# Another written order in the first segment, and other slots and pairs in the attention steps

## The chip, the cores and the metric

The kernel runs on one core of one Trainium2 chip. The time is device microseconds of that core. TensorE (PE) multiplies, VectorE (DVE), ScalarE (ACT) and GpSimd (POOL) do the elementwise work, and SyncE (SP) issues nearly all transfers. Each engine works through its own instructions in a fixed order, and an instruction that waits holds up everything behind it on that engine.

## What is computed

One transformer block with 2048 tokens of width 1024, in float32, whose two norms are modulated by a condition c:

```python
mod = (silu(c) @ w_mod).reshape(6, 1, 1024)          # sa, ca, ga, sb, cb, gb
h = layernorm(x) * (1 + ca) + sa
x = x + ga * attention(h)
h = layernorm(x) * (1 + cb) + sb
x = x + gb * ((gelu(h @ w_gate) * (h @ w_up)) @ w_down)
```

The attention has 32 heads of 32 and goes through the tokens in four segments s of 512. In each segment, with phi(t) = t + 1 for t > 0 and exp(t) else:

```python
a_dot = softmax(qs @ ks.T * scale + mask) @ vs       # within the segment, causal
a_mem = phi(qs) @ M / (phi(qs) @ z + 1e-6)           # from the segments before
o = g * a_mem + (1 - g) * a_dot                      # g = sigmoid(beta), per head
M = M + phi(ks).T @ vs ; z = z + sum(phi(ks))
```

Then o @ wo. So a segment reads the memory M, z that the segments before it have left.

## The kernel before

**Products.** A float32 operand is cut into a high part, rounded to the fp32r type that PE takes at full speed, and a low part, the remainder. A product is three fp32r matmuls: high by high, low by high, high by low. The names carry this: kh and kl, qh and ql, hha and hla, and w with two halves. ACT writes the high part, DVE or GpSimd subtracts for the low part (`split_w` does it for weights, GpSimd in four pieces of 256 columns).

**Steps.** The attention has 32 steps n = (half hf, head group g of 4 heads, segment s). In step n PE computes the scores S and the memory M of step n, the projections v, k, q of step n + 1 (`kv_part`, `q_part`) and the values (T, O, R) of step n − 1. What stands after what on PE is set by a string of 31 letters:

```python
ORDER = "K N K K V K V N K K V V K N V K S Q S V V Q S Q A S K M Q V V"
```

Each letter advances one generator to its next yield; a letter's position is called its slot. Besides, a list `todo` of (slot, function) has weight loads, weight cuts and columns done at a slot; a slot beyond the end falls into the next step. PE's order is exactly this written order. In the first segment (`start`) the order of all engines is the written one. In the steps the other engines' order is set by a scheduler, which places an instruction when it reckons it ready; `behind=True` keeps an instruction in written order on its engine.

**A step's pieces.** q leaves PSUM three ways: qh (ACT), ql (DVE, from qh), and for s > 0 phi(q) = pq (ACT exp into eq, DVE min, DVE max and add). k likewise into kh, kl and kn, whose transposes kT give pk = phi(k). v goes through vr (ACT) and the transposes vT into vx. The two PSUM banks named mm serve v, k and q in turn. kh, kl, qh, ql are sent by SP into ks and qs, 96 rows for the three matmul terms. S is masked and its row maximum taken by DVE (sj, mm), exponentiated for the sum by ACT (sj). The maxima go through a DVE transpose (tt) into rows 96 to 128 of qs, so that T = ks' qs comes with the maximum subtracted; ACT takes its exp (pt), GpSimd masks it, and O follows. rx and ry are the factors of the two parts: rx from the sums (ACT), ry from the memory's denominator (DVE), num is phi(q) by mz, the masked memory.

**Columns.** The modulation vector's rows 16 to 47 are computed in the steps, one or two per step: SP loads 128 rows of w_mod into a raw tile (`mod_load`, four raw tiles serve all loads), and one DVE instruction of 1024 elements (`mod_col`, L146) multiplies and sums them into a column of modT. In the first segment the columns that the first norm needs are made partly so and partly by PE (`mod_rows`, `mod_cols`).

**The first segment** normalises segment 0 on the chip: statistics per tile of 128 tokens on DVE, the power on GpSimd, scale on ACT and DVE, transposes on PE (`turn`), modulation on ACT (`high`), low part on DVE (`low`), then the products for q, k, v of step 0 k-tile by k-tile (`products`). The same is begun for segment 1 (x1), whose eight k-tiles `norm_seg` then finishes in step 0. `warm` issues matmuls whose result nobody reads.

## Time and profile before

| | us |
|---|---|
| median of 3 runs | 2773.78 |
| lowest and highest | 2773.21 and 2775.84 |
| the profiled execution | 2774.15 |
| its span | 2772.4 |
| PE busy in it | 2729.2 (98%) |
| DVE, ACT, POOL busy | 1767.3, 1287.7, 535.4 |

A row of a timeline has its start in us from the span's beginning, its duration in us, the engine, the line of the program, the instruction, what it writes from what, and in brackets how long the engine stood idle before it and what ended that. Neighbours on one engine overlap by a little, since the end of an instruction lies in the start of the next; the distance between starts is what an instruction costs its queue. A row of waits has the waiting instruction, what ended the wait, the total, the number and the longest. The first segment reaches to about 65 us, the steps to about 970 us, and the feed-forward part, which the change leaves alone, fills the rest.

### The profile page before, as it was taken

To read this page: it belongs to the slowest core of one execution; us is meant where nothing else is said; L and a number is where in the kernel's file an instruction comes from. 1 tells how busy PE (TensorE), PEld (TensorE's weight loads), DVE (VectorE), ACT (ScalarE), POOL (GpSimd) and SP (SyncE) were. 2 spreads that over 40 slices of the span, in tenths; PEclk is the share of its full clock that TensorE was granted. 3 is DMA by queue.
4 is the path that set the end of the run, shared out by engine and by line. 5 is a ranking of instruction groups with operands and counts; after the bars stand their busy time and mean duration, and the time that the engine had idled before them with its cause. 6 is when DMAs were issued, how large, how long until landed. Compare 5 with 4: busy or idle time off the path is not lost.

```text
span 2772.4 us, 38550 instructions
## 1 busy us (share of the span) xinstructions
PE 2729.2 (98%) x13336; PEld 2206.0 (80%) x13336; DVE 1767.3 (64%) x3723; ACT 1287.7 (46%) x2855; POOL 535.4 (19%) x972
## 2 busy tenths in 40 slices
PE   7999999999999999999999999999999999999999
PEld 5777777777777777788888887888888888888887
DVE  7565657767566754777776768667778754434552
ACT  6788866767676735334443324233223243232221
POOL 1333333333333521100000002000000002012442
PEclk9999999999999999999999999999999999999999
DMA  7666656665555657656555754333567595544652
GB/s 258 123 145 150 148 111 131 146 140 126 115 111 99 155 176 247 200 205 219 208 208 183 245 176 156 122 145 143 190 239 254 214 315 176 183 139 155 199 197 80
DMA packets 229748, 480.18 MB, mean 173 GB/s; under 512 B 17456, under 2 KB 92464, under 8 KB 229552
## 3 DMA queue, kind: packets, MB, share of 16 engines
q1 hardware_dynamic: 229408, 477.58, 57.3%
q8 instruction: 105, 1.72, 0.3%
q14 instruction: 91, 0.75, 0.1%
q10 hardware_dynamic: 144, 0.13, 0.0%
HBM read 300.96 MB, written 126.35 MB: 154 GB/s over the span
## 4 chain that ended last, share of the span: by engine, by line
PE 86%; DVE 6%; issue 2%; DMA 2%; ACT 2%; POOL 0%; SPq 0%; DVEq 0%; ACTq 0%; POOLq 0%
PE f L1286 36%; PE d L1457 19%; PE k L318 6%; PE q L318 5%; PE y L790 4%; PE v L318 3%; PE S L658 3%; PE O L731 3%; PE T L722 3%; DVE qs L675 1%; PE M L638 1%; DVE sj L660 1%; PE R L745 1%; PE num L696 1%; PE vT L334 0%
## 5 line engine op out<-in xcount | busy, mean ns | idle before, releaser
L1286 PE MATMUL f<-A,B 128*128 128x512 f32 x4704 | 1074.6, 390 | 4.8 <-DVE c L1251 3.2
L1286 PEld LDWEIGHTS f<-A,B 128*128 128x128 f32 x4704 | 882.3, 188 | 190.5 <-issue 2.9
L1457 PE MATMUL d<-wb,ah 128*128 128x512 f32 x2352 | 534.2, 389 | 0.2 <-DVE wb L1337 0.2
L1457 PEld LDWEIGHTS d<-wb,ah 128*128 128x128 f32 x2352 | 441.3, 188 | 92.7 <-DVE wb L1337 0.6
L660 DVE CUSTOM_DVE_ANT_0 sj<-S,mask 128x384 f32<-128x384 f32 (+3 forms) x512 | 227.8, 487 | 183.1 <-PE S L658 174.4
L662 ACT ACTIVATE sj<-sj,mm 128x384 f32<-128x384 f32 (+3 forms) x512 | 282.3, 556 | 28.1 <-DVE mm L660 26.0
L724 ACT ACTIVATE pt<-T 128x256 f32<-128x256 f32 (+3 forms) x512 | 184.9, 457 | 116.8 <-PE T L722 111.9
L725 POOL TENSOR_SCALAR_AFFINE_SELECT pt<-pt 128x128 f32<-128x128 f32 x512 | 168.3, 347 | 338.1 <-ACT pt L724 331.0
L1337 DVE TENSOR_TENSOR ah<-ar,ah 128x1792 fp32r<-128x1792 f32 x56 | 116.4, 2079 | 171.0 <-ACT ah L1336 163.5
L1336 ACT ACTIVATE ah<-ar 128x1792 fp32r<-128x1792 f32 x56 | 95.3, 1702 | 274.1 <-PE d L1457 248.2
L1253 ACT ACTIVATE g<-g 128x512 f32<-128x512 f32 x56 | 35.4, 632 | 302.8 <-DVE g L1253 302.8
L160 POOL TENSOR_TENSOR w<-r,w 128x256 fp32r<-128x256 f32 x180 | 133.1, 771 | 165.3 <-ACT w L155 144.9
L924 DVE TENSOR_TENSOR B<-t,B 128x512 fp32r<-128x512 f32 x168 | 116.1, 691 | 56.4 <-ACT B L927 56.3
L1362 POOL TENSOR_TENSOR yo<-u,gbb 128x256 f32<-128x256 f32 x32 | 30.0, 970 | 547.6 <-ACT gbb L132 547.6
L927 ACT ACTIVATE B<-t 128x512 fp32r<-128x512 f32 x168 | 105.5, 628 | 63.8 <-PE f L1286 60.0
L790 PE MATMUL y<-wo,hho 128*128 128x512 f32 x384 | 125.8, 393 | 0.5 <-DVE xr L794 0.5
L722 PE MATMUL T<-qs,ks 128*128 128x256 f32 (+2 forms) x512 | 115.0, 339 | 7.3 <-DVE qs L675 2.6
L722 PEld LDWEIGHTS T<-qs,ks 128*128 128x128 f32 x512 | 82.9, 188 | 48.4 <-issue 21.7
L1250 ACT ACTIVATE g<-f 128x512 f32<-128x512 f32 x56 | 33.5, 598 | 176.5 <-PE f L1286 176.5
L1380 POOL TENSOR_TENSOR xo<-xo,yo 128x256 f32<-128x256 f32 x64 | 71.8, 1151 | 210.7 <-DMA xo<-x_d 161.6
L924 DVE TENSOR_TENSOR B<-rg,B 128x512 fp32r<-128x512 f32 x112 | 78.2, 699 | 52.4 <-ACT B L927 52.2
L658 PE MATMUL S<-ks,qs 96*128 96x256 f32 (+2 forms) x512 | 108.3, 333 | 0.8 <-DVE mm L660 0.8
(251 smaller groups left out, 4326.5 us busy)
## 6 DMA issues: line engine op xcount, KB each, us to landing
ar<-hid_d SPq DMA_DIRECT2D x56, 896.0 KB, 5.1
rg<-wg SPq DMA_DIRECT2D x56, 512.0 KB, 4.6
ru<-wu SPq DMA_DIRECT2D x56, 512.0 KB, 5.4
hid_d<-g SPq DMA_DIRECT2D x56, 512.0 KB, 3.0
sc<-hid_d SPq DMA_DIRECT2D x56, 512.0 KB, 5.6
hid_d<-sc SPq DMA_DIRECT2D x56, 512.0 KB, 3.0
...
```

Source lines behind the costliest of these rows:

```text
L160: eng.tensor_sub(w[:, 1, k:k + 256], r[:, k:k + 256], f32(w[:, 0, k:k + 256]))
L318: nc.tensor.matmul(ps, w[:, a], b, start=(kt == 0 and a == 0 and b is hi), stop=(kt == KT - 1 and a == 1))
L658: nc.tensor.matmul(ps[:, :nk], qs[:96, j, i * P:(i + 1) * P], ks[:96, j, :nk], start=True, stop=True)
L660: nc.vector.tensor_tensor_reduce(out=sj[:, :nv], in0=ps[:, :nv], in1=mask[:, L - nv:], scale=-1.0, scalar=3.4e38, op0=ALU.add, op1=ALU.min ...
L662: nc.scalar.activation(sj[:, :nv], sj[:, :nv], AF.Exp, bias=mm[:, j, i:i + 1], scale=-1.0, accum_out=ll[:, i, j:j + 1])
L722: nc.tensor.matmul(ps[:, :nn], ks[:, j, kc * P:(kc + 1) * P], qs[:, j, L - nn:], start=True, stop=True)
L724: nc.scalar.activation(pt, ps[:, nn - n:nn], AF.Exp)
L725: nc.gpsimd.affine_select(pt[:, :P], pt[:, :P], pattern=[[1, P]], compare_op=ALU.is_ge, fill=0.0, base=0, channel_multiplier=-1)
L790: nc.tensor.matmul(ps, b[:, i * P:(i + 1) * P], w[:, a, g % 2], start=(g == 0 and a == 0 and b is hi), stop=(g == G - 1 and a == 1))
L924: eng.tensor_sub(dst[:, k], a[:, k], b[:, k])
L1286: nc.tensor.matmul(ps, B[m, i][:, a, kt * P:(kt + 1) * P], A[p, i, kt][b], start=(start and kt == 0 and a == 0 and b == 0), stop=(kt == 3 ...
L1457: nc.tensor.matmul(ps[t], ops[n][:, x, k, t * P:(t + 1) * P], b[:, y, kk % 2], start=(kk == 0 and x == 0 and y == 0), stop=(kk == 13 and x ...
```

## The change

Five things are edited.

1. In `start` the order is another. The statistics of tile 0 come ahead of the diagonal that spreads the condition, scales of segment 0 go to ACT in six of eight cases (four before), the cut of wv stands behind the modulation rows, k-tile 6 comes ahead of 4 and 5, and the four statistics of segment 1 stand together with the scales behind them. Ahead of k-tile 2 stand two warming matmuls where three were, and six more follow the last product. kl and ql are written after v's copy.
2. GpSimd's order in the first two steps is the written one.
3. In `k_out` kn comes ahead of kl, and in `q_out` eq ahead of ql.
4. `memory` yields after mz, and the string has one M more ahead of the third Q, so that mz is written there.
5. Weight cuts and loads have other slots (14, 19, 26, 37 become 15, 20, 24, 31), and a column comes 23 slots after its load and not 14.

Left out of the diff are helpers that only carry this (`stats`, `shift`, `scale` are the old statements one by one, and `SC` gets its entries in either order).

```diff
@@ -334,15 +336,19 @@
             nc.tensor.transpose(ps[:, t * P:(t + 1) * P], vr[:, t * P:(t + 1) * P], ident)
         nc.vector.tensor_copy(vx[:, :, :P], ps.rearrange("p (t m) -> p t m", m=P))
 
-    def k_out(s, nm, ps):
+    def k_low(kh, kl, ps):
+        nc.vector.tensor_sub(kl, ps, f32(kh))
+
+    def k_out(s, nm, ps, low=k_low):
         kh = t2("kh" + nm, "sp", bufs=4, dt=F32R)
         kl = t2("kl" + nm, "sp", bufs=4, dt=F32R)
         nc.scalar.activation(kh, ps, AF.Copy)
-        nc.vector.tensor_sub(kl, ps, f32(kh))
         kr = None
         if s < NSEG - 1:
             kr = t2("kn" + nm, "kn")
             nc.scalar.activation(kr, ps, AF.Copy)
+        if low:
+            low(kh, kl, ps)
         return kh, kl, kr
 
     def k_send(n, kh, kl, kr):
@@ -365,12 +371,13 @@
         qh = t2("qh" + nm, "sp", bufs=4, dt=F32R)
         ql = t2("ql" + nm, "sp" if n else "sj", bufs=4 if n else 3, dt=F32R)
         nc.scalar.activation(qh, ps, AF.Copy, scale=SCALE)
+        if s > 0:
+            e = tmp_tile("eq" + nm)
+            nc.scalar.activation(e, ps, AF.Exp)
         nc.vector.scalar_tensor_tensor(ql, ps, SCALE, f32(qh), op0=ALU.mult, op1=ALU.subtract)
         qs = t2("qs" + nm, "qs", bufs=2, dt=F32R, shape=(P, 4, L))
         pq = None
         if s > 0:
-            e = tmp_tile("eq" + nm)
-            nc.scalar.activation(e, ps, AF.Exp)
             nc.vector.tensor_scalar_min(e, e, 1.0)
             pq = t2("pq" + nm, "pq", bufs=2)
             nc.vector.scalar_tensor_tensor(pq, ps, 0.0, e, op0=ALU.max, op1=ALU.add)
@@ -472,32 +478,24 @@
...
-        def normal(halves, name, engs):
-            st = []
-            for i in range(4):
-                if i > 1:
-                    scale(i - 2, halves, *st[i - 2], name, engs)
-                st.append(norm_stats([halves[0][i], halves[1][i]], f"{name}{i}"))
-                yield
-            for i in (2, 3):
-                scale(i, halves, *st[i], name, engs)
-
-        for i, _ in enumerate(normal(x0, "a0", (nc.scalar, nc.vector))):
-            if i in (2, 3):
-                next(row)
...
@@ -555,14 +553,36 @@
                 for kt in kts:
                     mm(i, ps[i], 0, 0, kt)
 
+        (xa, xb), dve = x0, nc.vector
+        stats(0, 0, x0)
+        next(row)
+        shift(0, 0)
+        scale(xa[0], 0, 0)
+        scale(xb[0], 0, 0)
+        stats(0, 1, x0)
+        stats(0, 2, x0)
+        shift(0, 1)
+        scale(xa[1], 0, 1)
+        scale(xb[1], 0, 1)
+        stats(0, 3, x0)
+        shift(0, 2)
+        scale(xa[2], 0, 2)
+        nc.vector.tensor_reduce(sel4, pick, axis=AX.X, op=ALU.add)
+        nc.vector.tensor_copy(blk.rearrange("p (j e) -> p j e", e=DH), sel4.unsqueeze(2).to_broadcast([P, 4, DH]))
+        shift(0, 3)
+        scale(xa[3], 0, 3)
+        scale(xb[2], 0, 2, dve)
+        scale(xb[3], 0, 3, dve)
+        for _ in row:
+            pass
         warm(1)
-        cut(1)
         mod_rows(0, 0)
+        turn(0)
+        turn(1)
         warm(1)
         mod_rows(0, 1)
+        cut(1)
         warm(1)
-        turn(0)
-        turn(1)
         mod_cols(0)
         for d in range(4):
             nc.sync.dma_start(spare[d], wms[1, d])
@@ -576,7 +596,7 @@
         cut(0)
         turn(2)
         turn(3)
-        warm(3)
+        warm(2)
         high(2)
         mods(3)
         low(2)
@@ -585,43 +605,54 @@
         nc.sync.dma_start(bb, bass.AP(tensor=beta.tensor, offset=beta.offset, ap=[[0, P], [1, H]]))
         x1 = [fetch(x[L + i * P:L + (i + 1) * P, :], f"x1_{i}") for i in range(4)]
         x1h = [[t[:, h * L:(h + 1) * L] for t in x1] for h in range(2)]
-        norm = normal(x1h, "a1", (nc.vector, nc.scalar))
         products(0, 1)
         mod_rows(1, 0)
         products(2)
         high(3)
         low(3)
+        turn(6)
+        mods(6)
         mod_rows(1, 1)
+        high(6)
         turn(4)
+        mod_cols(1)
         turn(5)
-        mod_col(*got[6][0])
-        mod_cols(1)
         high(4)
-        mod_col(*got[6][1])
         products(3)
         high(5)
-        low(4)
-        turn(6)
         mod_col(*got[7][0])
-        low(5)
-        high(6)
+        low(6)
         mod_col(*got[7][1])
-        low(6)
-        products(4)
         turn(7)
         high(7)
-        next(norm)
+        products(6)
+        low(4)
+        low(5)
+        stats(1, 0, x1h)
+        low(7)
+        stats(1, 1, x1h)
+        shift(1, 0)
+        scale(x1h[0][0], 1, 0)
+        scale(x1h[1][0], 1, 0)
+        products(4)
         products(5)
-        low(7)
-        products(6, 7)
-        next(norm)
-        kk = k_out(0, nm, ps[2])
+        products(7)
+        stats(1, 2, x1h)
+        shift(1, 1)
+        scale(x1h[0][1], 1, 1)
+        stats(1, 3, x1h)
+        shift(1, 2)
+        kk = k_out(0, nm, ps[2], None)
+        warm(6)
+        scale(x1h[0][2], 1, 2)
+        shift(1, 3)
+        scale(x1h[0][3], 1, 3)
+        for i in range(1, 4):
+            scale(x1h[1][i], 1, i, dve)
+        vv = v_out(0, nm, ps[1])
+        k_low(*kk[:2], ps[2])
         k_send(0, *kk)
         q_out(0, 0, nm, ps[0])
-        next(norm)
-        vv = v_out(0, nm, ps[1])
-        for _ in norm:
-            pass
         k_turn(0, 0, nm, *kk)
         v_turn(nm, *vv)
         sigmoid(gall, bb)
@@ -690,7 +721,7 @@
             mz = t2("mz" + nm, "mz", bufs=1, shape=(P, P + 4))
             nc.vector.tensor_mul(mz[:, :P], M[:, :P], blk)
             nc.vector.tensor_scalar_mul(mz[:, P:], sel4, M[:, P:P + 1])
-
+            yield
             ps = [s_ps(f"num{nm}_{i}").rearrange("p (i m) -> p i m", i=2)[:, :, :P + 4] for i in range(2)]
             for i in range(4):
                 nc.tensor.matmul(ps[i // 2][:, i % 2], pq[:, i * P:(i + 1) * P], mz, start=True, stop=True)
@@ -1491,7 +1522,7 @@
 
 
     steps = [(hf, g, s) for hf in range(2) for g in range(G) for s in (2 * hf, 2 * hf + 1)]
-    ORDER = "K N K K V K V N K K V V K N V K S Q S V V Q S Q A S K M Q V V"
+    ORDER = "K N K K V K V N K K V V K N V K S Q S V V Q M S Q A S K M Q V V"
     ORDER0 = "N N N N N N N N K K K K S K S K S K A S K Q Q Q K M Q"
     none = iter(())
     todo = []
@@ -1504,7 +1535,11 @@
             norm_1 = start()
         norm_a = norm_tiles(x, hT_d, (2, 3), 1, 0, "a")
         next(norm_a)
+        firsts = ExitStack()
+        firsts.enter_context(tc.manual_schedule(engines={mybir.EngineType.Pool}))
         for n in range(len(steps) + 1):
+            if n == 2:
+                firsts.close()
             work = {k: none for k in "VSAMKQN"}
             if n > 0:
                 work["V"] = values(n - 1, *steps[n - 1][1:])
@@ -1526,7 +1561,7 @@
             else:
                 work["K"] = work["Q"] = proj
             if n + 2 < len(steps) and n % 2 == 0:
-                weights(*steps[n + 2][:2], [(4, 0, 1), (8, 0, 2), (14, 1, 1), (19, 1, 2), (26, 0, 0), (37, 1, 0)])
+                weights(*steps[n + 2][:2], [(4, 0, 1), (8, 0, 2), (15, 1, 1), (20, 1, 2), (24, 0, 0), (31, 1, 0)])
             if n == 30:
                 rs = {}
 
@@ -1542,7 +1577,7 @@
                 for pos in (20, 27)[:1 + (15 <= n < 20)]:
                     got = []
                     todo.append((pos, lambda r=rest.pop(0), got=got: got.append(mod_load(r))))
-                    todo.append((pos + 14, lambda got=got: mod_col(*got[0], behind=True)))
+                    todo.append((pos + 23, lambda got=got: mod_col(*got[0], behind=True)))
             for pos, q in enumerate((ORDER if n else ORDER0).split()):
                 for f in [f for at, f in todo if at == pos]:
                     f()
```

DVE at the end of the first segment, from ql and the scales of segment 1 (rx here, with their statistics sta, mva, rsa and shifts mra) on. Before:

```order
L341 TENSOR_TENSOR kl0_0_504<-k0_0_241,kh0_0_503 128x512
L368 SCALAR_TENSOR_TENSOR ql0_0_513<-q0_0_242,qh0_0_512 128x512
L480 TENSOR_SCALAR mra1_0_520<-mva10_460,rsa10_464 128x1
L484 TENSOR_SCALAR rx1_0_333<-rx1_0_333,rsa10_464,mra1_0_520 128x512
L191 BN_STATS sta12_524<-rx1_2_337 128x6 x2
L194 BN_AGGR mva12_525<-sta12_524 128x2
L196 TENSOR_SCALAR rsa12_529<-mva12_525 128x1
L480 TENSOR_SCALAR mra1_1_536<-mva11_496,rsa11_500 128x1
L484 TENSOR_SCALAR rx1_1_335<-rx1_1_335,rsa11_500,mra1_1_536 128x512
L191 BN_STATS sta13_540<-rx1_3_339 128x6 x2
L194 BN_AGGR mva13_541<-sta13_540 128x2
L196 TENSOR_SCALAR rsa13_545<-mva13_541 128x1
```

With the change:

```order
L489 TENSOR_SCALAR mra1_1_514<-mva1_1_468,rsa1_1_472 128x1
L193 BN_STATS sta1_3_517<-rx1_3_338 128x6 x2
L196 BN_AGGR mva1_3_518<-sta1_3_517 128x2
L198 TENSOR_SCALAR rsa1_3_522<-mva1_3_518 128x1
L489 TENSOR_SCALAR mra1_2_525<-mva1_2_507,rsa1_2_511 128x1
L489 TENSOR_SCALAR mra1_3_540<-mva1_3_518,rsa1_3_522 128x1
L495 TENSOR_SCALAR rx1_1_334<-rx1_1_334,rsa1_1_472,mra1_1_514 128x512
L495 TENSOR_SCALAR rx1_2_336<-rx1_2_336,rsa1_2_511,mra1_2_525 128x512
L495 TENSOR_SCALAR rx1_3_338<-rx1_3_338,rsa1_3_522,mra1_3_540 128x512
L340 TENSOR_TENSOR kl0_0_528<-k0_0_181,kh0_0_527 128x512
L377 SCALAR_TENSOR_TENSOR ql0_0_555<-q0_0_182,qh0_0_554 128x512
L365 TENSOR_SCALAR ek0_0_567<-ek0_0_567 128x512
```

kl and ql stood ahead of the first scale, and each scale stood between two sets of statistics. Now the statistics of all four tiles are through first (the first two lie further up), then the last shifts, three scales, and only then kl and ql.

ACT at the end of a step of the first half, where q of group 1, segment 1 is taken out of PSUM (pt are the exponentials of step 1, 0). Before:

```order
L358 ACTIVATE ek1_1_1630<-kT1_1_1625 128x512
L367 ACTIVATE qh1_1_1641<-q1_1_1493 128x512
L682 ACTIVATE rx1_0_1618<-rc1_0_1615 128x512
L373 ACTIVATE eq1_1_1646<-q1_1_1493 128x512
L724 ACTIVATE pt1_0_00_1695<-T1_0_00_1693 128x512
```

With the change:

```order
L364 ACTIVATE ek1_1_1639<-kT1_1_1634 128x512
L373 ACTIVATE qh1_1_1650<-q1_1_1502 128x512
L376 ACTIVATE eq1_1_1653<-q1_1_1502 128x512
L713 ACTIVATE rx1_0_1629<-rc1_0_1626 128x512
L755 ACTIVATE pt1_0_00_1709<-T1_0_00_1707 128x512
```

eq stood between rx and the first pt; now it stands ahead of rx, right behind qh.

DVE at the end of a step of the second half, around pq of group 2, segment 2 (wm38 is a column, mz2_2 the small part of the masked memory, vx2_3 the next values). Before:

```order
L368 SCALAR_TENSOR_TENSOR ql2_2_7993<-q2_2_7840,qh2_2_7992 128x512
L753 TENSOR_TENSOR R1_2_7877<-R1_2_7877,Y1_2_8005 128x512
L146 ISA wm38_7875,modT_108<-wm38_7875,scb_110 128x1024
L146 ISA modT_108 128x1
L374 TENSOR_SCALAR eq2_2_7997<-eq2_2_7997 128x512
L151 TENSOR_SCALAR modT_108<-modT_108 128x1
L692 TENSOR_SCALAR mz2_2_8333<-sel4_100,Mt2_1_2738 128x4
L376 SCALAR_TENSOR_TENSOR pq2_2_8000<-q2_2_7840,eq2_2_7997 128x512
L335 COPY vx2_3_8064<-vT2_3_8101 128x4x128
```

With the change:

```order
L377 SCALAR_TENSOR_TENSOR ql2_2_8002<-q2_2_7847,qh2_2_8001 128x512
L381 TENSOR_SCALAR eq2_2_8004<-eq2_2_8004 128x512
L784 TENSOR_TENSOR R1_2_7886<-R1_2_7886,Y1_2_8014 128x512
L383 SCALAR_TENSOR_TENSOR pq2_2_8009<-q2_2_7847,eq2_2_8004 128x512
L723 TENSOR_SCALAR mz2_2_8267<-sel4_100,Mt2_1_2750 128x4
L337 COPY vx2_3_8071<-vT2_3_8108 128x4x128
L146 ISA wm38_7884,modT_108<-wm38_7884,scb_110 128x1024
L146 ISA modT_108 128x1
L151 TENSOR_SCALAR modT_108<-modT_108 128x1
```

The column wm38 stood ahead of eq and pq; now it stands behind vx, and pq follows two rows after eq.

More of the change, by code (lines that the diff above doesn't have):

```diff
@@ L151, in mod_col, with split_w @@
             nc.vector.tensor_scalar_add(modT[:, r:r + 1], modT[:, r:r + 1], 1.0)
-    def split_w(r, w, eng=nc.gpsimd):
-        nc.scalar.activation(w[:, 0], r, AF.Copy)
+    def split_w(r, w, eng=nc.gpsimd, behind=False):
+        i = nc.scalar.activation(w[:, 0], r, AF.Copy)
+        if behind:
+            tc.keep_in_program_order(i)
         if eng is nc.vector:
@@ L307, in cut @@
         def cut(i):
-            W[g][i] = split_w(raws[i], wsp_tile(f"w{i}_{half}_{g}"))
+            W[g][i] = split_w(raws[i], wsp_tile(f"w{i}_{half}_{g}"), behind=False)
         for pos, f, i in at:
@@ L472, in warm, with stats, shift, scale @@
                 nc.tensor.matmul(ps[:, :2 * P], ones, mask[:, :2 * P], start=True, stop=True)
-        nc.vector.tensor_reduce(sel4, pick, axis=AX.X, op=ALU.add)
-        nc.vector.tensor_copy(blk.rearrange("p (j e) -> p j e", e=DH), sel4.unsqueeze(2).to_broadcast([P, 4, DH]))
-        def scale(i, halves, mv, rs, name, engs):
-            mr = cs([P, 1], f"mr{name}_{i}", tag="mr", bufs=4)
-            nc.vector.tensor_scalar(mr, mv[:, 0:1], rs, -1.0, op0=ALU.mult, op1=ALU.mult)
-            for h in range(2):
-                t = halves[h][i]
-                if engs[h] is nc.vector:
-                    nc.vector.tensor_scalar(t, t, rs, mr, op0=ALU.mult, op1=ALU.add)
-                else:
-                    nc.scalar.activation(t, t, AF.Identity, bias=mr, scale=rs)
-        def normal(halves, name, engs):
-            st = []
-            for i in range(4):
-                if i > 1:
-                    scale(i - 2, halves, *st[i - 2], name, engs)
-                st.append(norm_stats([halves[0][i], halves[1][i]], f"{name}{i}"))
-                yield
-            for i in (2, 3):
-                scale(i, halves, *st[i], name, engs)
-        for i, _ in enumerate(normal(x0, "a0", (nc.scalar, nc.vector))):
-            if i in (2, 3):
-                next(row)
+        st = {}
+        def stats(s, i, halves):
+            st[s, i] = norm_stats([halves[0][i], halves[1][i]], f"a{s}_{i}")
+        def shift(s, i):
+            mv, rs = st[s, i]
+            mr = cs([P, 1], f"mra{s}_{i}", tag="mr", bufs=4)
+            nc.vector.tensor_scalar(mr, mv[:, 0:1], rs, -1.0, op0=ALU.mult, op1=ALU.mult)
+            st[s, i] = rs, mr
+        def scale(t, s, i, eng=nc.scalar):
+            rs, mr = st[s, i]
+            if eng is nc.vector:
+                nc.vector.tensor_scalar(t, t, rs, mr, op0=ALU.mult, op1=ALU.add)
+            else:
+                nc.scalar.activation(t, t, AF.Identity, bias=mr, scale=rs)
         w0 = W[0] = [None] * 3
@@ L543, in high @@
             nc.scalar.activation(hi[kt][1], h, AF.Copy)
-        hT[0] = []
+        hT[0] = [None] * KT
         def low(kt):
@@ L682, in scores @@
         nc.scalar.activation(rx, rc.unsqueeze(3).to_broadcast([P, 4, 4, DH]), AF.Copy)
-        SC[n] = [rx, None]
+        SC.setdefault(n, [None, None])[0] = rx
     def memory(n, g, s):
```

4 lines of the change are left out of this document (2 added, 2 removed).

## The prediction

> **What bounds the kernel now.** I read the windows by stage first, to see where TensorE stands still at all.
>
> ```profile
> 40.00:60.00 20.00, 14.85 (x76) 12.00 (x76) 16.15 (x40) 13.02 (x22) 2.67 (x7) 0.91 0.68 94
> ...
> 300.00:600.00 300.00, 293.82 (x1710) 230.47 (x1709) 198.41 (x661) 212.84 (x614) 112.40 (x249) 1.00 0.64 138
> 600.00:970.00 370.00, 363.52 (x2096) 283.69 (x2095) 247.44 (x829) 256.00 (x734) 138.15 (x302) 1.00 0.58 120
> 970.00:2772.00 1802.00, 1790.10 (x7964) 1475.65 (x7962) 1125.83 (x1614) 591.45 (x938) 195.78 (x208) 1.00 0.55 191
> ```
>
> The columns are the stretch, its length, then busy time of PE, weight load, DVE, ACT, POOL, the granted clock, DMA share and GB/s. After 970 us, where the change touches nothing, PE is full. Between 40 and 60 it idles 5.15 us, and through the attention steps some 6 us in 300 and again in 370. So the kernel is bound by TensorE, and only its stalls can be won. Then the list of PE's waits, for who ends them:
>
> ```profile
> PE k L318 <- ACT vr L325: 3.4, 7, 0.5
> PE tpa L282 <- DVE rx L484: 3.2, 3, 2.0
> ...
> PE T L722 <- DVE qs L675: 2.6, 4, 0.8
> PE T L722 <- DVE ry L704: 2.4, 5, 0.9
> ...
> PE T L722 <- ACT pt L724: 1.7, 3, 0.8
> ...
> PE kT L356 <- ACT kn L345: 1.3, 1, 1.3
> ...
> PE k L318 <- DVE pq L376: 0.7, 2, 0.3
> ```
>
> Each row gives the total, the number of waits and the longest. None is large; the change aims at the queues of ACT and DVE behind six of them, so I take them one by one.
>
> **The first segment: its beginning loses.** These are ACT and, last, DVE between 17 and 20 us:
>
> ```profile
> 17.57 1.06 ACT L155 ACTIVATE w<-rw 128x1024 fp32r<-128x1024 f32 x1 [1.02 <-DMA rw<-wv]
> 18.53 0.58 ACT L519 ACTIVATE mr<-md 128x512 f32<-128x512 f32 x1
> 20.57 0.78 ACT L541 ACTIVATE h<-tpa,modT 128x512 f32<-128x512 f32 x1 [1.47 <-DVE modT L526]
> 18.66 1.23 DVE L157 TENSOR_TENSOR w<-rw,w 128x1024 fp32r<-128x1024 f32 x1 [2.38 <-ACT w L155]
> ```
>
> Before, the cut of wv (1.06 on ACT, 1.23 on DVE) runs while PE still makes the modulation rows. The change puts that cut behind mr, and eight transposes ahead of the second half of the rows. By my reckoning mr then starts at 18.35 (18.53 now), the cut at 18.85, its DVE half at 19.95, and modT, behind it on DVE, at 21.2; the first h goes from 20.57 to 21.45. Some of this 0.9 is made up, since the order of the eight k-tiles is better packed; I carry 0.6 to the last product, with 0 and 0.9 as bounds.
>
> **Its end gains.** The timelines of ACT, DVE and PE around the start of segment 1:
>
> ```profile
> 45.51 0.60 ACT L345 ACTIVATE kn<-k 128x512 f32<-128x512 f32 x1 [0.83 <-DVE kl L341]
> 54.32 1.49 ACT L284 ACTIVATE h<-tpa,modT 128x512 f32<-128x512 f32 x2
> ...
> 40.94 1.28 DVE L191 BATCH_NORM_STATS2 sta<-rx 128x6 f32<-128x512 f32 x2
> ...
> 50.27 1.28 DVE L191 BATCH_NORM_STATS2 sta<-rx 128x6 f32<-128x512 f32 x2
> ...
> 51.90 0.20 DVE L480 TENSOR_SCALAR mra<-mva,rsa 128x1 f32<-128x1 f32 x1
> ...
> 53.00 0.55 DVE L484 TENSOR_SCALAR rx<-rx,rsa,mra 128x512 f32<-128x512 f32 x1
> ...
> 65.50 0.65 PE L658 MATMUL S<-ks,qs 96*128 96x256 f32 x4
> ```
>
> Now the last scale of the next segment's tokens ends at 53.55, because kl, ql and the scales stand between the statistics on DVE. After the change the four statistics follow each other from about 41.5 (40.94 and the 0.6 lost above), each 1.63 long (50.27 to 51.90), with one hla (0.6) and small shifts (0.9) between, then three scales of 0.46: the end is at about 51, and ACT, which has the other half of each tile and waits for the last shift only, comes to its first h at 51.7 instead of 54.32: a gain of 2.6. From there to the first S at 65.50 the chain is ACT's two passes over each of eight k-tiles, unchanged, so S moves up by the same 2.6. The cover of that is the transfer of q: ql is sent some 5 us later than now, and I expect the last qs to land about 1.2 us before S asks for it. If it came 2 us later, 0.8 would be lost. The six extra warming matmuls fall where PE waits anyway.
>
> In step 0 two more stalls go:
>
> ```profile
> 80.06 0.60 ACT L345 ACTIVATE kn<-k 128x512 f32<-128x512 f32 x1 [1.18 <-DVE kl L341]
> 84.16 0.60 ACT L373 ACTIVATE eq<-q 128x512 f32<-128x512 f32 x1 [0.76 <-DVE ql L368]
> 90.32 0.44 PE L722 MATMUL T<-qs,ks 128*128 128x384 f32 x1 [0.69 <-ACT pt L724]
> ```
>
> kn and eq need only the product in PSUM, but the program makes ACT wait for the DVE subtraction written ahead of them. With kn straight behind kh its 1.3 us on PE (the kT row above) goes. eq 0.76 earlier brings the normalisation of the next tokens forward as well, and of the T stall of 0.69 I count 0.4 as won. The first segment and step 0: 2.6 + 1.3 + 0.4 = **4.3 won**; bounds 2 and 6.
>
> **k behind pq (A).** Nine times k waits 0.3 to 0.5 by the list. The lateness is more, since the ends of matmuls are modelled:
>
> ```profile
> 608.92 0.87 PE L722 MATMUL T<-qs,ks 128*128 128x384 f32 x4
> 609.62 0.40 PE L318 MATMUL k<-hhh,w 128*128 128x512 f32 x1
> ...
> 636.76 0.69 PE L722 MATMUL T<-qs,ks 128*128 128x384 f32 x3
> 637.91 0.50 PE L318 MATMUL k<-hhh,w 128*128 128x512 f32 x1 [0.46 <-ACT vr L325]
> ...
> 635.58 1.27 DVE L146 CUSTOM_DVE_ANT_0 wm<-wm,scb 128x1024 f32<-128x1024 f32 x1
> 637.39 0.68 DVE L376 SCALAR_TENSOR_TENSOR pq<-q,eq 128x512 f32<-128x512 f32 x1
> ...
> 647.08 0.29 DVE L660 CUSTOM_DVE_ANT_0 sj<-S,mask 128x128 f32<-128x128 f32 x1 [3.29 <-PE S L658]
> ```
>
> Undisturbed, four T take 0.70 to the next k; three would put k at 637.28, and it starts at 637.91: 0.6 late. k needs one of two PSUM banks, the one that q leaves when pq has read it, or the one that v leaves with vr. pq stands behind a column of 1.27 on DVE, so the program gave k the bank of v. In the change the column stands behind pq and vx, k gets the bank of q everywhere, and pq, 1.2 us earlier, ends near 636.8, 0.5 before k asks. Nine times 0.6 is **5.4 won**; nothing at the other end, if pq only exchanges the column for another delay.
>
> **T behind qs (B).**
>
> ```profile
> 316.30 2.71 DVE L675 TENSOR_SCALAR qs<-tt,seli 32x512 fp32r<-32x512 f32 x4
> 317.12 3.46 POOL L160 TENSOR_TENSOR w<-r,w 128x256 fp32r<-128x256 f32 x4 [5.11 <-ACT w L155]
> 490.89 1.69 DVE L675 TENSOR_SCALAR qs<-tt,seli 32x512 fp32r<-32x512 f32 x4
> ```
>
> The four qs take 1.69 alone and 2.71 beside GpSimd's part of a weight cut. In two steps eq now goes ahead of that cut on ACT, GpSimd starts 0.5 later, and about half of the 0.8 stall goes: 1.0. In a third a column leaves the chain to qs, and the whole 0.9 goes. In the fourth the cut only moves from before rx to before pt and wins nothing. Together **1.9**, bounds 0 and 2.6.
>
> **T behind pt (C).** In seven steps eq stands between rx and the first pt and waits for ql:
>
> ```profile
> 144.71 0.60 ACT L373 ACTIVATE eq<-q 128x512 f32<-128x512 f32 x1 [0.30 <-DVE ql L368]
> ```
>
> 0.30 idle and 0.49 for eq itself hold every pt back, and PE loses about 0.3, in three of them 0.6: 3.0 by the starts of T against their usual distance. With eq done before rx, pt starts 0.8 to 0.9 earlier, more than the lateness. I take **2.6**, bounds 0 and 3.0. T behind ry stays: ry keeps its place.
>
> **What is added.** The M token ahead of Q, for mz: in the order of DVE mz hardly moves, so nothing. GpSimd's order in the first two steps: nothing on PE's path. Two weight cuts of the second half of the steps (1.05 each, ACT) come to stand between rx and pt, and part of each shows: 0.8. In five steps a second column now falls between the fourth and fifth sj of the scores; what follows there on DVE has idle time of over 1 us a little later, so 0.1 each, 0.5. Bounds 0 and 6 (five columns and a cut in full). The sum is −4.3 − 5.4 − 1.9 − 2.6 + 1.3 = −12.9 us, against the profiled execution's 2774.15 (span 2772.4): 2761.25, and as that execution is 0.37 above the median of 2773.78, **2761 us**.
>
> **A rule against it.** The columns' own length varies, and the wait for raw tiles has a measured scale:
>
> ```profile
> L146 DVE CUSTOM_DVE_ANT_0 wm<-wm,scb x32: 1158/1217/1725, 119.5 to 863.4; 128x1024 f32<-128x1024 f32 x32
> ...
> 644.21 0.33 SPq L97 DMA_DIRECT2D r<-wv  x1
> ...
> 648.23 1.04 ACT L155 ACTIVATE w<-r 128x1024 fp32r<-128x1024 f32 x1
> ...
> DMA to landing us min/median/max: 3.4/4.4/5.6
> ```
>
> The Trainium skill, page "GPSIMD Engine Reference", section "1. Specifications", says that GpSimd's way to SBUF is shared with VectorE and is contended by VectorE instructions that read two SBUF inputs. A column reads two, and the change puts it behind vx, where GpSimd masks the pt and splits weights. The trace's spread of the column, 1.22 in the middle and 1.73 at most, agrees with it. By this rule, taken at its worst, rival 2 below is the result; by the rows alone it is the sum above.
>
> **The rivals.** (1) The stalls of A and C come back under another name: the next thing due is pt or vr, 0.5 behind at most, so PE runs into it. For: these waits are all within 0.5 of each other. Against: pq and eq move by more than that. Then the first segment and half of the rest remain: 4.3 + 5.0 − 1.3 = 8.0, 2766.
> (2) The columns, moved beside GpSimd's work, are all as long as the longest, 0.5 more for each of 32: 16 us if each lay on the path, so 2777. Against: DVE has 3.29 idle before the next scores (the row at 647.08), which hides it.
> (3) Slower: a column nine slots later (a step has 31 slots and takes 28.3 us, from the k at 609.62 to that at 637.91, so up to 8.2 us) keeps its raw tile, one of four, and the next weight load on SP's queue waits for it, with the sends of k and q behind that. ACT, in order, then stands at the cut with kh, kn and pt behind it, and PE at kT. It decides once a load is issued less than its landing time, 3.4 to 5.6, ahead of the cut; the load at 644.21 and its cut at 648.23 have 4.0 now. Seven loads of the second half wait for a column, and about 4 us each would be 28 less the 13: 2789. Against: the order shows the columns moved past only a few DVE instructions in steps with one column.
> (4) More is won: T behind ry goes too (2.4 by the list), since DVE runs ahead, and B and C reach their upper bounds (1.1): 2757.5.
> (5) The edit of the columns does not do what it says, because the scheduler, not the slot, sets DVE's order; the order after shows that it does, at pq.
>
> **How the numbers follow.** A measurement here tells about 0.2%, 5.5 us, from no change: faster means below 2768.3, slower above 2779.3. The forecast has 0.58 (2757 to 2767), rival 1 0.15, rival 4 0.10, rival 2 0.08, rival 3 0.07, rival 5 0.02. Faster: forecast, rival 4 and most of rival 1, 0.81. Same: the rest of rival 1, rival 5 and most of rival 2, 0.11. Slower: 0.08. The range 2754 to 2771 takes in rivals 1 and 4 and leaves out the two long sides.
>
> **What would show it.** Right: the first h of segment 1 at about 51.7 and the first S at about 62.9; no kT wait for kn; the rows of k behind vr and pq gone from PE's list; T behind pt down to one or two; T behind ry as now. Wrong: PE's list names the DMA of qs at the first S, or ACT's list names the DMA of a weight at the cuts, or the idle time between 300 and 970 us stays at 12 us with other names.

## The result, and the profile after

| | before | after |
|---|---|---|
| median of 6 runs (us) | 2773.57 | 2754.44 |
| lowest and highest | 2772.83 to 2775.84 | 2752.35 to 2757.19 |
| the profiled execution, its span | 2774.15, 2772.4 | 2753.47, 2751.7 |

The ratio is 0.9932, with an interval of 0.9922 to 0.9942: faster by 19.1 us between the medians. The forecast was 2761, 12.6 below this median of before. The direction held and the time lies at the low edge of the range of 2754 to 2771; a third of the gain was not foreseen.

The windows by stage of the kernel after, with the same columns as before:

```profile
40.00:60.00 20.00, 18.95 (x99) 14.41 (x97) 16.35 (x39) 16.08 (x27) 2.57 (x6) 1.00 0.67 87
...
300.00:600.00 300.00, 297.93 (x1742) 237.04 (x1742) 199.58 (x681) 216.46 (x618) 108.44 (x251) 1.00 0.62 136
600.00:970.00 370.00, 368.25 (x2129) 287.51 (x2128) 254.71 (x838) 260.67 (x743) 139.67 (x304) 1.00 0.58 127
```

Of the 12.7 us that PE stood still between 300 and 970, 3.8 are left. These are waits of PE in the kernel after, all in the steps:

```profile
PE S L689 <- DVE mm L691: 1.7, 4, 0.7
PE T L753 <- DVE ry L735: 1.4, 2, 0.8
...
PE vT L336 <- ACT pt L755: 1.0, 3, 0.4
PE R L776 <- DVE mm L691: 0.9, 2, 0.5
PE T L753 <- ACT pt L755: 0.8, 2, 0.6
```

The rows of k behind vr and pq, of T behind qs, of kT behind kn and of tpa behind rx are gone. T behind ry, which was to stay, went from five waits of 2.4 to two of 1.4. S and R behind mm grew, from 0.8 and 0.5 to 2.6 together; 1.0 of that is S in step 0.

To place the gain I use one mark: the start of the first S of a step. These rows of PE's timeline are the first S of step 1 and of step 31 before,

```profile
99.33 0.64 PE L658 MATMUL S<-ks,qs 96*128 96x256 f32 x4
...
962.91 0.64 PE L658 MATMUL S<-ks,qs 96*128 96x256 f32 x4
```

and after:

```profile
95.13 0.64 PE L689 MATMUL S<-ks,qs 96*128 96x256 f32 x4
...
943.72 0.64 PE L689 MATMUL S<-ks,qs 96*128 96x256 f32 x4
```

So the kernel after is 4.2 ahead when step 1 starts, and 19.2 ahead at step 31: the steps themselves take 848.6 in place of 863.6, 15.0 less. What follows step 31 is the same program in both and took 1808.0 and 1809.5.

The leads flatter the change by about 1 us, because the profiled execution of before began late. Its first h, the first modulated tile on ACT, starts at 20.57. In the six variants below that keep the old order of the first segment the first h starts at 19.44 to 19.88; in cols_only at

```profile
19.80 0.78 ACT L541 ACTIVATE h<-tpa,modT 128x512 f32<-128x512 f32 x1 [1.46 <-DVE modT L526]
```

In that one execution of before PE waited until 12.46 for its first modulation weights (11.29 to 11.71 in the six). So each lead below is 0.7 to 1.1 too large, an estimate from these rows. The lengths of the steps, and differences between two variants, are not touched by it.

Where the 15.0 went is read from PE's groups between these marks, shapes kept apart: busy time, mean ns, then idle time before them. A late matmul shows in both, since ends are modelled, so I add the two. Before:

```profile
L318 PE MATMUL k<-hhh,w 128*128 128x512 f32 x256 | 88.2, 395 | 3.4 <-ACT vr L325 3.4
L318 PE MATMUL k<-hha,w 128*128 128x512 f32 x209 | 72.4, 397 | 0.7 <-DVE pq L376 0.7
...
L722 PE MATMUL T<-qs,ks 128*128 128x512 f32 x120 | 36.1, 408 | 5.9 <-DVE qs L675 2.6 <-DVE ry L704 2.4 <-ACT pt L724 0.8
L722 PE MATMUL T<-qs,ks 128*128 128x384 f32 x120 | 29.3, 350 | 0.5
```

After:

```profile
L320 PE MATMUL k<-hhh,w 128*128 128x512 f32 x256 | 87.4, 392 | 0.0
L320 PE MATMUL k<-hha,w 128*128 128x512 f32 x209 | 72.3, 396 | 0.0
...
L753 PE MATMUL T<-qs,ks 128*128 128x512 f32 x120 | 35.8, 406 | 1.6 <-DVE ry L735 1.4
...
L753 PE MATMUL T<-qs,ks 128*128 128x384 f32 x120 | 26.2, 339 | 0.0
```

The counts agree, so the sums can be compared. k: 4.1 idle gone and 0.9 shorter in these two groups, 4.8 over all matmuls of k. The 512-wide T, the first four of a step's values, from 42.0 to 37.4: 4.6. The 384-wide T, the next four, from 29.8 to 26.2: 3.6. Against that S and R together are 1.1 longer; O, num, tpa and kT are 1.7 shorter, q is 0.4 longer, and 1.8 remain that no group shows.

Why does T wait less behind ry? One step of the second half shows it. Before, on ACT, GpSimd, DVE and PE:

```profile
659.42 1.05 ACT L155 ACTIVATE w<-r 128x1024 fp32r<-128x1024 f32 x1
663.15 0.60 ACT L373 ACTIVATE eq<-q 128x512 f32<-128x512 f32 x1 [2.68 <-DVE ql L368]
...
660.55 3.32 POOL L160 TENSOR_TENSOR w<-r,w 128x256 fp32r<-128x256 f32 x4 [8.32 <-ACT w L155]
...
659.72 2.17 DVE L675 TENSOR_SCALAR qs<-tt,seli 32x512 fp32r<-32x512 f32 x4
...
663.61 0.89 PE L722 MATMUL T<-qs,ks 128*128 128x512 f32 x2 [0.38 <-DVE ry L704]
```

The same step after:

```profile
646.60 0.58 ACT L376 ACTIVATE eq<-q 128x512 f32<-128x512 f32 x1
647.07 1.05 ACT L155 ACTIVATE w<-r 128x1024 fp32r<-128x1024 f32 x1
...
648.20 4.85 POOL L162 TENSOR_TENSOR w<-r,w 128x256 fp32r<-128x256 f32 x6 [8.47 <-ACT w L155]
...
646.89 1.70 DVE L706 TENSOR_SCALAR qs<-tt,seli 32x512 fp32r<-32x512 f32 x4
...
649.79 1.42 PE L753 MATMUL T<-qs,ks 128*128 128x512 f32 x4
```

eq now uses the 0.5 us in which ACT used to begin the weight cut. So GpSimd's half of the cut, which waits for ACT's, starts 1.3 after the first qs and not 0.8. Three of the four qs are through by then: they take 1.70 and not 2.17, and everything behind them on DVE, ry among it, is 0.47 earlier. ry kept its place in the order; it did not keep its time.

### The profile page after: what moved, and what is told of

The parts are those of the page before. It is cut to its first block, busy times and chain, and to the rows that moved or that the text cites. A ratio compares the mean times of both kernels' runs of the same rounds, so it can differ in the third digit from the quotient of the medians.

```text
span 2751.7 us, 38558 instructions
## 1 busy us (share of the span) xinstructions
PE 2721.7 (99%) x13346; PEld 2206.5 (80%) x13346; DVE 1756.6 (64%) x3720; ACT 1289.0 (47%) x2858; POOL 523.5 (19%) x972
## 4 chain that ended last, share of the span: by engine, by line
PE 90%; DVE 4%; ACT 2%; DMA 2%; issue 2%; POOL 1%; SPq 0%; DVEq 0%; POOLq 0%; ACTq 0%
PE f L1317 36%; PE d L1488 19%; PE k L320 6%; PE y L821 6%; PE q L320 6%; PE v L320 5%; PE T L753 3%; PE O L762 3%; PE S L689 3%; PE num L727 1%; PE M L669 1%; PE R L776 1%; PE vT L336 1%; DVE A L955 0%; ACT sj L693 0%
## 5 line engine op out<-in xcount | busy, mean ns | idle before, releaser
L756 POOL TENSOR_SCALAR_AFFINE_SELECT pt<-pt 128x128 f32<-128x128 f32 x512 | 150.5, 313 | 315.9 <-ACT pt L755 308.7
L162 POOL TENSOR_TENSOR w<-r,w 128x256 fp32r<-128x256 f32 x180 | 140.7, 812 | 177.4 <-ACT w L155 175.8
```

Source lines behind the costliest of these rows:

```text
L162: eng.tensor_sub(w[:, 1, k:k + 256], r[:, k:k + 256], f32(w[:, 0, k:k + 256]))
L756: nc.gpsimd.affine_select(pt[:, :P], pt[:, :P], pattern=[[1, P]], compare_op=ALU.is_ge, fill=0.0, base=0, channel_multiplier=-1)
```

## Experiments

Every kernel was timed beside the kernel before on the same chip (its medians there were 2772.6 to 2773.6). "Lead" is how much earlier than before the first S of a step starts. T and k are busy and idle time of all their matmuls between the first S of step 1 and that of step 31 (before: 114.2 and 255.8).

| run | median | ratio, interval | lead at step 1 | lead at step 31 | T | k |
|---|---|---|---|---|---|---|
| the change | 2754.44 | 0.9932 (0.9922 to 0.9942) | 4.2 | 19.2 | 106.0 | 251.0 |
| start_only | 2773.78 | 0.9999 (0.9990 to 1.0009) | −0.8 | −1.2 | 114.8 | 255.8 |
| swap_only | 2758.69 | 0.9945 (0.9930 to 0.9960) | 2.9 | 14.1 | 105.7 | 254.5 |
| eq_only | 2760.44 | 0.9956 (0.9942 to 0.9971) | 0.9 | 12.7 | 106.4 | 254.3 |
| kn_only | 2771.90 | 0.9996 (0.9987 to 1.0006) | 2.7 | 1.7 | 113.6 | 257.3 |
| cols_only | 2768.85 | 0.9983 (0.9974 to 0.9992) | 0.8 | 3.9 | 114.0 | 250.9 |
| no_split | 2761.54 | 0.9960 (0.9945 to 0.9975) | 0.5 | 12.4 | 104.9 | 256.1 |
| steps_only | 2754.93 | 0.9932 (0.9917 to 0.9947) | 2.9 | 16.3 | 106.2 | 251.0 |
| no_kn | 2757.19 | 0.9943 (0.9926 to 0.9960) | 2.6 | 17.6 | 106.3 | 250.9 |
| no_cols | 2756.72 | 0.9947 (0.9933 to 0.9962) | 3.9 | 14.5 | 106.6 | 254.3 |
| no_rest | 2761.96 | 0.9959 (0.9944 to 0.9974) | 0.4 | 13.5 | 104.6 | 251.0 |
| pin_first | 2756.27 | 0.9939 (0.9925 to 0.9954) | 3.8 | 18.2 | 106.0 | 251.0 |
| pin_all | 2758.55 | 0.9953 (0.9936 to 0.9969) | 3.8 | 16.6 | 106.8 | 251.1 |

The leads come from one profiled execution each, against the one of before that began 0.7 to 1.1 late; the medians are from 4 to 10 runs. So a lead at step 1 of under 1 us says nothing by itself.

### The first segment alone (start_only)

The kernel before with edit 1 only; kl stays ahead of kn.

```diff
-        norm = normal(x1h, "a1", (nc.vector, nc.scalar))
...
+        stats(1, 2, x1h)
+        shift(1, 1)
+        scale(x1h[0][1], 1, 1)
+        stats(1, 3, x1h)
+        shift(1, 2)
+        kk = k_out(0, nm, ps[2], None)
+        warm(6)
```

> Only the first segment of the change; in the steps kl stays ahead of kn and ql ahead of eq, columns 14 slots on. Theory (each edit takes away its own stalls, the gains add): the first scores at 61.3 us as with the whole change (65.5 before), the steps as before, so 4.2 us less than before: about 2769.4. Rival (the lead is eaten in step 0, because the queue of ACT there sets the end and kn still waits for kl): the lead falls below 2 us by the scores of step 1, time 2772.

Measured 2773.78: no change. The first S of step 0 starts at 61.26, 4.2 early, exactly as in the full change; by step 1 the lead is gone and 0.8 more. PE's waits of this run say where:

```profile
PE kT L360 <- ACT kn L349: 3.5, 1, 3.5
...
PE S L686 <- DVE mm L688: 1.9, 4, 0.7
```

PE comes earlier to kT, and the wait of 1.3 for kn grows to 3.5. These are the load and ACT there:

```profile
74.20 0.33 SPq L97 DMA_DIRECT2D r<-wv  x1
...
74.50 0.58 ACT L343 ACTIVATE kh<-k 128x512 fp32r<-128x512 f32 x1
78.47 1.06 ACT L155 ACTIVATE w<-r 128x1024 fp32r<-128x1024 f32 x1 [3.39 <-DMA r<-wv]
79.43 0.58 ACT L349 ACTIVATE kn<-k 128x512 f32<-128x512 f32 x1
```

What holds kn last is not kl, which DVE has done at 77.88, but a weight cut that stands between kh and kn. Its load was issued at 74.20 and ACT waits 3.39 for it to land. It is the fourth cut in step 0; the kernel before and the change have three there, and their fourth comes at 105.37 and 98.93. Without it kn could have started at 77.88 and not at 79.43. So the first segment's gain is real at its own end and worth nothing alone: step 0 takes it back, at kT, at S behind mm, and with a granted clock of 0.92 between 80 and 100 us (1.00 before).

### The two swaps together (swap_only)

The kernel before with edit 3.

```diff
+        if s > 0:
+            e = tmp_tile("eq" + nm)
+            nc.scalar.activation(e, ps, AF.Exp)
         nc.vector.scalar_tensor_tensor(ql, ps, SCALE, f32(qh), op0=ALU.mult, op1=ALU.subtract)
```

> Only the two pairs: kn ahead of kl, eq ahead of ql. Theory: T behind pt (4.0 us by lateness) goes, two of the T behind qs lose half (1.0), the kT wait of step 0 (1.3) goes; k behind vr or pq stays: 6 us less, about 2767.5. Rival (pt and k bind within half a us of each other, so what one wait gives back the next takes): less than 3 us, 2771 or more.

Measured 2758.69, 14.3 below the kernel before on that chip: three quarters of the gain, and far more than my theory gave it. T falls by 8.5, as much as in the full change. k keeps its wait under another name:

```profile
PE k L318 <- DVE pq L381: 3.3, 4, 1.5
```

Before it was 3.4 behind vr and 0.7 behind pq. Here k gets q's bank, and pq still stands behind a column. So the swaps are T's cure, not k's.

### eq alone and kn alone (eq_only, kn_only)

Each is one of the two swaps on the kernel before.

```diff
         nc.scalar.activation(kh, ps, AF.Copy)
-        nc.vector.tensor_sub(kl, ps, f32(kh))
...
+        if low:
+            low(kh, kl, ps)
```

The lines above are kn_only; eq_only is the diff of swap_only.

> Only eq ahead of ql. Theory as it now stands: eq on ACT goes ahead of the weight cut, GpSimd's part of the cut starts 0.5 us later and leaves qs alone, and eq no longer holds pt and pq; that is what the two pairs won behind step 1, about 12 us: 2761. Rival (kn ahead of kl brings the lead, since kh, kn and kl stand at the same place in every step): less than 7 us, 2766 or more.

> Only kn ahead of kl. Theory: 2.9 us, the first segment and step 0 (the only kT that waits for kn in the list), nothing after: 2770. Rival (the lead of the two pairs is kn's): 2765 or less.

eq_only: 2760.44, 12.7 less than before. kn_only: 2771.90, which its interval doesn't tell from no change; by the trace it is 2.7 ahead at step 1 (2.0 if counted from the first h, which leaves the late beginning of before out) and loses 1.0 of that again in the steps, where k's waits behind pq grow. T's groups of eq_only:

```profile
L723 PE MATMUL T<-qs,ks 128*128 128x512 f32 x120 | 35.3, 404 | 2.7 <-DVE qs L676 1.3 <-ACT pt L725 0.8 <-DVE ry L705 0.6
...
L723 PE MATMUL T<-qs,ks 128*128 128x384 f32 x120 | 26.0, 338 | 0.0
```

38.0 and 26.0: of the 8.2 that T lost in the full change, eq alone gives 7.8.

### GpSimd's half of the weight cuts taken away (no_split)

The kernel before, with a fill of zeros in place of the four subtractions. So the low parts of the weights for q, k, v and o are missing from the products; the matmuls and transfers are as before.

```diff
-        for k in range(0, 1024, 256):
-            eng.tensor_sub(w[:, 1, k:k + 256], r[:, k:k + 256], f32(w[:, 0, k:k + 256]))
+        eng.memset(f32(w[:, 1]), 0.0)
```

> The kernel before, in which GpSimd's four subtractions for the low part of a weight are replaced by writing zeros (so the weights' low parts are left out of the products). Theory (GpSimd's reading and writing slows qs on DVE, and ql, ry and T stand behind that): the waits of T for qs and ry, 5.0 us in the list of before, fall under 1.5 us, and the time by 5 to 6 us: 2768. Rival (qs is not what T waits for behind ry; that wait is DVE's own queue): T behind ry stays at 2 us or more, 2770.

Measured 2761.54, 11.6 below before, twice what I had put on it. The mean of one qs between 120 and 970 us, in the kernel before,

```profile
L675 DVE TENSOR_SCALAR qs<-tt,seli 32x512 fp32r<-32x512 f32 x116 | 55.0, 532 | 0.8
```

in the kernel after,

```profile
L706 DVE TENSOR_SCALAR qs<-tt,seli 32x512 fp32r<-32x512 f32 x120 | 50.8, 482 | 0.8
```

and in no_split, with its T:

```profile
L674 DVE TENSOR_SCALAR qs<-tt,seli 32x512 fp32r<-32x512 f32 x120 | 50.8, 481 | 0.8
...
L721 PE MATMUL T<-qs,ks 128*128 128x512 f32 x120 | 33.1, 394 | 0.9 <-DVE qs L674 0.5 <-ACT pt L723 0.3
L721 PE MATMUL T<-qs,ks 128*128 128x384 f32 x120 | 28.2, 347 | 0.3
```

Without the subtractions qs takes 481 ns on average, and with the change 482: the change removes all of the slowing that GpSimd causes there. GpSimd is also free sooner for the mask of pt in no_split, but PE waited for that mask only 0.2, before and here alike, so that is not what was won. The 512-wide T falls by 8.0 (42.0 to 34.0), by more than with the change; the 384-wide only by 1.3 (29.8 to 28.5), since here eq still stands between rx and pt. This separates the two ways in which eq's place acts: on the first T through GpSimd's start and DVE, on the next T through ACT's own order.

### The columns (cols_only, no_cols)

One number, in the kernel before and, the other way, in the change:

```diff
-                    todo.append((pos + 14, lambda got=got: mod_col(*got[0], behind=True)))
+                    todo.append((pos + 23, lambda got=got: mod_col(*got[0], behind=True)))
```

> Only the columns 23 slots behind their loads instead of 14. Theory: all of k behind vr and pq (5.6 us by lateness), one T behind qs (0.9) and the T behind ry of the second half (up to 3) go: 6.5 to 9.5 us less, 2764 to 2767. Rival (the columns beside GpSimd get longer and hold DVE): the columns' middle length rises from 1.22 to over 1.5 us and the time is 2773 or more.

> The whole change, but columns 14 slots behind their loads, as before. Theory (early eq already brings pq early in most steps, so the columns only add where a column stood between eq and pq or ahead of qs): 2 to 3 us more than the whole change, about 2757. Rival of the prediction (the nine waits of k behind pq are won by the columns): 5.4 us more or above, 2760.

cols_only: 2768.85, 4.1 below before, less than expected. k's waits are gone (255.8 to 250.9, 4.9), T stays at 114.0, and a part goes to a wait that was 0.8 before:

```profile
PE S L658 <- DVE mm L660: 1.4, 3, 0.5
```

no_cols: 2756.72, 2.3 above the change. Its trace has k waiting again:

```profile
PE k L320 <- DVE pq L383: 3.2, 4, 1.5
```

and a lead 4.7 smaller at step 31. The steps themselves are 3.1 shorter in cols_only than before, and 4.3 longer in no_cols than in the change: that is what the columns are worth there. The medians of no_cols and the change differ by less; their intervals overlap.

### The change with the old first segment (steps_only), and with kl ahead of kn (no_kn)

```diff
         nc.scalar.activation(kh, ps, AF.Copy)
+        if low:
+            low(kh, kl, ps)
         kr = None
```

The lines above are no_kn against the change; steps_only keeps the old `start`, the other way round from start_only.

> The whole change but for the written order of the first segment, which is that of before. Theory (gains add): the 19.1 us of the change less the 4.2 of the first segment: about 2758.6. Rival (the first segment's order is needed for the step's gains): 2762 or more.

> The whole change, but kl stays ahead of kn in the steps. Theory: the lead of 4.2 us of the first segment needs kn early; without it kT of step 0 waits over 3 us as with the first segment alone, and the time is 4 to 5 us above the whole change, 2758.5 to 2759.5. Rival (kn is worth only the wait that the profile of before shows, 1.3): 2755.7.

steps_only: 2754.93, only 0.5 above the change, where I expected about 4. Its first S of step 0 is at 63.85 with the old order, 1.65 ahead of before, of which 1.1 is the late beginning of before. Its lead at step 1 is 2.9, which kn_only has too (2.7). So with kn early, the new first segment adds 1.3 at step 1 and 2.9 at step 31 by the trace, and 0.5, within the spread, by the medians; the two ratios are the same. no_kn: 2757.19, 2.75 above the change, between theory and rival; kT waits 1.3 for kn again, and the lead at step 1 is 2.6. The theory's wait of over 3 did not come; no fourth cut stands ahead of kn here.

### Without the three small edits (no_rest)

The change without the early M, the new slots of the weights, and GpSimd's written order.

```diff
-            yield
...
-        firsts.enter_context(tc.manual_schedule(engines={mybir.EngineType.Pool}))
...
-                weights(*steps[n + 2][:2], [(4, 0, 1), (8, 0, 2), (15, 1, 1), (20, 1, 2), (24, 0, 0), (31, 1, 0)])
+                weights(*steps[n + 2][:2], [(4, 0, 1), (8, 0, 2), (14, 1, 1), (19, 1, 2), (26, 0, 0), (37, 1, 0)])
```

> The whole change without its three small edits: the M that is written earlier, the other slots of the weight cuts, GpSimd's written order in the first steps. Theory: the orders hardly differ, so within 1 us of the whole change, 2753.5 to 2755.5. Rival (they carry the 2.5 us that the steps of the change won beyond the two pairs): 2757 or more.

Measured 2761.96, 7.5 above the change: the theory, that they do nothing, missed. 3.8 of it is lost in step 0. ACT and PE of no_rest there:

```profile
78.27 1.06 ACT L155 ACTIVATE w<-r 128x1024 fp32r<-128x1024 f32 x1 [2.87 <-DMA r<-wv]
...
86.03 1.24 ACT L206 ACTIVATE na<-na,mra,rsa 128x1024 f32<-128x1024 f32 x1 [2.84 <-DVE mra L204]
...
87.81 1.10 PE L753 MATMUL T<-qs,ks 128*128 128x384 f32 x2 [2.86 <-ACT pt L755]
```

and of the change:

```profile
64.39 1.06 ACT L155 ACTIVATE w<-r 128x1024 fp32r<-128x1024 f32 x1 [0.80 <-DMA r<-wv]
67.32 1.99 ACT L155 ACTIVATE w<-r 128x1024 fp32r<-128x1024 f32 x2
...
83.85 1.25 ACT L206 ACTIVATE na<-na,mra,rsa 128x1024 f32<-128x1024 f32 x1 [0.56 <-DVE mra L204]
...
85.63 0.93 PE L753 MATMUL T<-qs,ks 128*128 128x384 f32 x2 [0.59 <-ACT pt L755]
```

Without the edits the fourth cut stands in step 0 again, as in start_only, and waits 2.87 for its load. With kn early it now holds ek (the exponential for phi(k)), which starts at 79.24 and not at 77.00. DVE's work behind ek, up to the statistics of the next tokens, is about as much later; their normalisation (na) waits 2.84 for it, with three pt behind, and PE's T waits 2.86. PE's granted clock is 0.91 there between 80 and 100 us, and 1.00 in the change. In the change ACT waits at most 0.80 for a load, at an earlier cut, and na and T wait 0.56 and 0.59. Another 1.9 goes between step 1 and step 31, mostly at S. The rest of the 7.5 lies behind step 31, where the edits change nothing. Which of the three edits keeps the fourth cut out of step 0 was not tried apart.

### Weight cuts kept at their written places (pin_first, pin_all)

The change, with the cuts of step 0 alone, or of all steps, held in written order on ACT.

```diff
-            W[g][i] = split_w(raws[i], wsp_tile(f"w{i}_{half}_{g}"), behind=False)
+            W[g][i] = split_w(raws[i], wsp_tile(f"w{i}_{half}_{g}"), behind=half == 0 and g == 1)
```

In pin_all the argument is `behind=True`.

> The whole change, and the three weight cuts of step 0 kept at their written places on ACT. Now the first cut stands ahead of the second four scores and waits 0.8 us for its load, and the other two stand back to back ahead of the third four; PE loses 1.8 us at the scores by lateness. Theory: that goes, and up to 1 us comes at pt, where the last cut then stands: 0 to 1.8 us less than the whole change, 2753 to 2754.5. Rival (the sum of ACT's work up to pt sets the end of step 0, wherever the cuts stand): the same as the whole change or 1 us more.

> The whole change, and all weight cuts of the steps kept at their written slots on ACT: one behind the last pt, one ahead of the third four scores, one between eq and rx, in every step pair; none between rx and pt. Theory (GpSimd's part of a cut slows qs where it falls on it, and a cut between rx and pt holds pt): qs stays at its undisturbed length, the three waits of vT for pt (1.0 us in the list) go: 1 to 3 us less than the whole change, 2751.5 to 2753.5. Rival (written slots are too early for the loads, and ACT stands at the cuts): ACT waits for loads of weights, and the time is 2757 or more.

pin_first: 2756.27, no better than the change. The waits of S fall from 1.7 to 0.7, and T behind pt has one of 2.9 in their place. It is as long as in no_rest, but here a held cut of 1.04 stands between na and the pt. pin_all: 2758.55, 4.1 above the change; its waits:

```profile
PE T L753 <- ACT pt L755: 3.2, 2, 2.9
PE S L689 <- DVE mm L691: 3.1, 4, 1.6
```

The wait of T is the one of pin_first, and S waits 1.4 more than in the change; what holds mm up there I did not follow further. No version beat the change.

## Why the prediction was right, and where it was short

At step 31 the trace has a lead of 19.2, some 18 to 18.5 without the late beginning of before, where the sum had 12.9. Term by term:

**What bounds the kernel: right.** The gain is PE's idle time and the hidden lateness of its matmuls, in the stages named, and nothing in the rest.

**First segment and step 0, 4.3: 4.2 in the trace, 3.1 to 3.5 without the late beginning of before, and made of other parts.** ACT, DVE and PE of the kernel after:

```profile
20.13 0.78 ACT L539 ACTIVATE h<-tpa,modT 128x512 f32<-128x512 f32 x1 [1.43 <-DVE modT L524]
50.11 1.45 ACT L286 ACTIVATE h<-tpa,modT 128x512 f32<-128x512 f32 x2
...
47.51 1.45 DVE L495 TENSOR_SCALAR rx<-rx,rsa,mra 128x512 f32<-128x512 f32 x3
...
61.26 0.65 PE L689 MATMUL S<-ks,qs 96*128 96x256 f32 x4
```

"Its beginning loses" looks wrong beside the 20.57 of before, since the first h is at 20.13. Beside the six other executions with the old order (19.44 to 19.88) it is right: 0.3 to 0.7 are lost, where I carried 0.6. The end gained more than I had: from the first h to the first S before took 44.93 and after 41.13, 3.8 less, where my 2.6 and the 0.6 make 3.2. So h of segment 1 comes at 50.11, not 51.7; the scales are done at 48.96, not 51; the first S is at 61.26, not 62.9. But the 1.3 of kT and the 0.4 of T in step 0 did not come on top: kT's wait went, and S waited 1.0 behind mm, and T still 0.59 behind pt, in the same step, which took 33.87 where it took 33.83. The early segment itself is worth little: start_only and steps_only give it between nothing and 2.9. What I had not seen is that kn alone gives about 2 at step 1 (kn_only), and that a fourth cut can come into step 0 and eat into the lead. The small edits together keep it out: without them the lead at step 1 is 0.4 and not 4.2, without kn early 2.6.

**k behind pq (A), 5.4: 4.8 measured.** Right in size and in cause: cols_only and no_cols put it on the columns, and with eq moved alone k waits for pq. By the length of the steps the columns are worth 3.1 (cols_only) to 4.3 (no_cols); in cols_only S and R take a part back.

**T behind qs (B), 1.9, and "T behind ry stays: ry keeps its place": 4.6 together.** This is the step that failed. I had the mechanism, eq ahead of the cut delays GpSimd, and applied it to two steps with a stall at qs, at half its size. The mean of qs, 482 with the change and 481 without any subtraction, says that the slowing went in all steps, and the step shown above that all that DVE does after qs moves with it. The place of ry in the order said nothing about its time. no_split shows the cause: take GpSimd's subtractions away and this T gains 8.0. The 4.6 go by the shape of T and also hold the 0.8 that the 512-wide T waited for pt before.

**T behind pt (C), 2.6: 3.6 measured,** by the 384-wide T, and a little over the upper bound of 3.0, probably for the same reason: in the step shown above rx starts 3.06 after the first qs (646.89 and 649.95), and before 3.93 (659.72 and 663.65), more than eq's length. no_split, in which eq keeps its place, gives this T 1.3.

**Added, 1.3: 1.1 measured,** S and R behind mm. cols_only alone adds 2.3 (S 1.9, R 0.4), and the change without the columns (no_cols) 0.1, so it is mainly the columns, which I had put at 0.5.

**"GpSimd's order in the first two steps: nothing", and the M token: "nothing".** As a group with the slots of the weights, wrong by 5.7 at step 31 (no_rest). My working looked only at what these edits move in the kernel before; 3.8 of their worth is that they let the other edits' lead through step 0.

The remaining 3.1 of the steps (O, num, tpa, kT, q and what no group shows) had no term in the sum.

**The rivals.** Rival 1 (the stalls come back) is true of start_only and in part of step 0, not of the steps. Rival 2: the columns' longest is 1.76 after and 1.73 before with the same middle of 1.22. Their mean rose from 1.25 to 1.31, 1.9 us for all 32 where the rival had 16, and cols_only is faster: it fell. Rival 3: in the change ACT waited 0.80 for a load once, in step 0. In start_only and no_rest it waited 3.39 and 2.87, at a cut whose load landed 4.2 after its issue, and in start_only with kn behind it and PE at kT, as the rival says. No column held the tile there, but the rest of the mechanism exists and took part of the lead of start_only; in the change it did not decide. Rival 5 fell. Rival 4 (2757.5) was nearest: its terms for T (2.4, 2.6 and 3.0, 8.0 together) meet the 8.2 measured. The 3.1 of the steps without a term is about what it lacks.
